# Seeding a PSUM bank from ScalarE and adding two matmul groups to it in one bank, in a fused Fourier mixing and gated feed-forward kernel

## The chip, the cores and the metric

The kernel runs on one core of one Trainium2 chip. The metric is the device time of one execution in microseconds (us). The kernel before took 1993.21 us, the median of three runs (1992.69 to 1993.93).

## The reference

```
X = np.fft.fft(x, axis=1); X = np.fft.fft(X, axis=2); attn_out = X.real     # x: (8, 3008, 256)
t = attn_out.reshape(8 * 3008, 256)
gate = 1 / (1 + exp(-(t @ w_gate)));  val = t @ w_val                       # (256, 1536) each
out = (gate * val) @ w_out                                                  # (1536, 256)
```

All data are float32. The real part of the two-dimensional transform has a symmetry that the kernel uses. With P the part made of cosines over both axes, Q the part made of sines over both axes, and E the part that comes from one feature column (the one in the middle), row k of a batch, times the weights, is P + E + Q, and row S - k is P + E - Q (S = 3008). So only 1505 rows of each batch are transformed, and each gives two rows of the result.

## The kernel before

**Weights.** The transform over the features is merged into the weights: for each of six pairs of blocks of 128 hidden features, `merge` multiplies the cosine table (`dt`) with a column block of w_gate or w_val in a PSUM bank (`ps`), and ScalarE copies the halves to `G2` and `G1`. Row 0 of `G2` is also sent by DMA into the small table `ge`, one column per block of 128 features; `ge` is the factor of E. The weights come as 64-bit numbers. `weight_parts` (two ScalarE operations) and `weight_join` (three VectorE operations and one on GpSimd, L236) turn a block of them into float32. `weight_load` brings the next block, and its buffer is that of an earlier block, so its DMA, which waits in the queue of SyncE, waits for that block's join. The `ge` transfers stand in the same queue behind it. `forms` makes seven combinations of the blocks of w_out, `wf`.

**Transform over the sequence.** For each batch, `half` sums products of a table of cosines or sines (`st`) with the folded input (`x`) into two PSUM banks, `ev` and `od`. ScalarE copies `ev` to `a` and `places` (VectorE) writes sums and differences of both to the rows of `pk` (P), `qk` (Q) and, for batch 0, `ek` (E). For batch 0 this is done ahead of the loop, with the groups of `cos` and `sin`. For batch b + 1 it is done in the middle of batch b (`whole`), at a unit where a chunk has just ended. E of batches 1 to 7 comes from `e_sums`, once.

**The main loop.** A batch's 1505 rows are cut into six chunks (five of 256 columns and one of 225). A chunk has six pairs, a pair has two blocks of 128 hidden features, and one block in one chunk is a unit: 8 x 6 x 12 = 576 units. A unit has three stages:

- `front` multiplies P by `G1` into bank `pa` and Q by `G2` into bank `pb`, gate and value side by side. VectorE computes `ae` = ge * ek + pa (L447, one operation for gate, one for value), then ae + pb for row k (L450) and ae - pb, in reversed order, for row S - k (L451), into `z`.
- ScalarE takes the sigmoid of the gate half of `z` (L672). `gate`, one unit later, multiplies gate and value into `h` (L462), and GpSimd makes sums of the parts of `h` in `s` (L464 to L468).
- `back`, two pairs later, multiplies `h` and `s` with `wf` into four PSUM banks `po`: seven products for a pair, three in its first unit and four in its second. At the end of a chunk ScalarE copies the four banks to `c` (L491, L549), GpSimd combines them, VectorE transposes (L509), and SyncE stores.

There are eight PSUM banks: a ring of four (pool `psx`) for `pa`, `pb`, `ps`, `ev`, `od` and `pe`, and four (`pso`) for `po`. The order of each engine's work is the order of the calls in the loop at the end of the kernel, written out by hand: `front` of a unit, `gate` of the unit before, `back`, the weight preparation (`pre`), the sigmoid, one step of the output work of the last chunk (`later`), and the rest of what is planned for that unit (`side`: joins, weight loads, merges, folds, transforms). Weight preparation fills the first units: units 0 to 8 each end with one merge, and the first `back` is that of unit 4. The `ps` of the merge for the gate of pair c stands in unit 2c - 3, that for its value in unit 2c - 2.

Of the kernel before, what the change touches and what calls it, by code (L numbers as in the profile page):

```python
# [42 lines left out]
NQ = 6  # L45
# [6 lines left out]
def kernel(  # L52
# [10 lines left out]
    nc = tc.nc  # L63
    B, _, _, _, D = xf.shape
    F = moe_w_gate.shape[1]
    P = 128
# [6 lines left out]
    NPR = NFT // 2  # L73
    CH = 256
# [15 lines left out]
    app = ctx.enter_context(tc.tile_pool(name="app", bufs=3))  # L90
    zp = ctx.enter_context(tc.tile_pool(name="zp", bufs=3))
# [3 lines left out]
    op = ctx.enter_context(tc.tile_pool(name="op", bufs=2))  # L95
    psx = ctx.enter_context(tc.tile_pool(name="psx", bufs=4, space=PSUM))
    pso = ctx.enter_context(tc.tile_pool(name="pso", bufs=1, space=PSUM))

    def mm(o, l, r, start, stop):
        nc.tensor.matmul(o, l, r, start=start, stop=stop, skip_group_check=True)  # L100
# [239 lines left out]
    PQE = {}  # L340

    def half(w, d, blk, sn, other=None):


        c0, n = ((0, NE), (NE, NO))[blk]
        ev, od = [bank(name, other and other[i])[:, 0:n] for i, name in enumerate(("ev", "od"))]

        def sums(*qs):
            for q in sorted(qs, key=lambda q: q % 2):
                mm((ev, od)[q % 2], w(q), ST[0][0:NP, int(sn), q, c0 : c0 + n], q < 2, q >= NQ - 2)  # L350

        def both():

            for r in range(2 - blk):
                for q in range(N3 if blk == 0 else NQ):
                    for par, sum_ in enumerate((ev, od)):
                        rows = slice(par * HP, par * HP + HP - 1 - (par and q % N3 == N3 - 1))
                        ks = slice(None) if blk else slice(r, n, 2)
                        wq = q if blk else q + N3 * (r ^ int(sn))
                        mm(sum_[:, ks], w(wq)[rows], ST[0][rows, int(sn), q, c0 : c0 + n][:, ks],  # L360
                           q == 0 and r == 0, q == (NQ if blk else N3) - 1)

        def then():
# [24 lines left out]
    def seq_group(b, blk, what, other=None):  # L388
        return half(lambda q: W[b, blk][what][:, q, :], PQE[b][what], blk, what == 1, other)
# [42 lines left out]
    def front(p, fh):  # L432
        b, c, i = pairs[p]
        k0, n = chunks[c]
        ks = slice(k0, k0 + n)
        f = 2 * i + fh
        fs = slice(f * P, (f + 1) * P)
        pk, qk, ek = PQE[b]
        pa = bank("pa").rearrange("p (g n) -> p g n", g=2)[:, :, 0:n]
        pb = bank("pb").rearrange("p (g n) -> p g n", g=2)[:, :, 0:n]  # L440
        for g in range(2):
            mm(pa[:, g], G1[:, g, fs], pk[:, ks], g == 0, True)
        for g in range(2):
            mm(pb[:, g], G2[:, g, fs], qk[:, ks], g == 0, True)
        ae = app.tile([P, 2, CH], F32, name="ae", tag="ae")[:, :, 0:n]
        for g in range(2):
            nc.vector.scalar_tensor_tensor(out=ae[:, g], in0=ek[:, ks], scalar=ge[:, g, f : f + 1],  # L447
                                           in1=pa[:, g], op0=ALU.mult, op1=ALU.add)
        z = zp.tile([P, 2, 2, CH], F32, name="z", tag="z")[:, :, :, 0:n]
        nc.vector.tensor_tensor(z[:, :, 0], ae, pb, op=ALU.add)  # L450
        nc.vector.tensor_tensor(z[:, :, 1, ::-1], ae, pb, op=ALU.subtract)  # L451
        return p, fh, z

    def gate(p, fh, z):

        n = chunks[pairs[p][1]][1]
        tt = nc.gpsimd.tensor_tensor
# [3 lines left out]
        h, s = H[p], SF[p]  # L461
        nc.vector.tensor_tensor(h[:, fh], z[:, 0], z[:, 1], op=ALU.mult)  # L462
# [14 lines left out]
    def back(p, part):  # L477
        b, c, i = pairs[p]
        n = chunks[c][1]
        if part == 0 and i == 0:  # L480
            PO[:] = [pso.tile([P, 2, CH], F32, name=f"po{t}", tag=f"po{t}") for t in range(4)]
        h, s = H[p], SF[p]
        move = {1: h[:, 0, 0], 2: h[:, 1, 0], 3: s[:, 3], 4: h[:, 1, 1], 5: s[:, 0], 6: s[:, 1],
                7: s[:, 2]}
        for m in ORDER[part]:
            t, j = SLOT[m]
            mm(PO[t][:, j, 0:n], wf[:, i, m - 1], move[m], i == 0 and m in FIRST,
               i == NPR - 1)
        if part == 0 and i == NPR - 1:
            PO.append(cp.tile([P, 7, CH], F32, name="c7", tag="c7"))  # L490
            nc.scalar.copy(PO[4][:, 6, 0:n], PO[3][:, 0, 0:n])  # L491
# [118 lines left out]
    def at(i, *fs):  # L610
        side.setdefault(i, []).extend(fs)

    def split(i, f, *args):

        at(i, lambda: at(i + 1, f(*args)))

    pre = {}
# [5 lines left out]
    for j in range(3, len(jobs)):  # L625
        w, c = jobs[j]
# [4 lines left out]
    i0 = 2 * NPR  # L631
# [7 lines left out]
    for i, f in enumerate(mirror_tables()):  # L639
        at(2 * i0 - 2 + i, f)  # L640
    at(3 * i0, e_fold)
    split(3 * i0 + 3, e_sums)
    at(3 * i0 + 5, table_again)

    for b in range(B - 1):
# [13 lines left out]
            for i, f in zip(calm(s0 if b else 3 * i0), mirror_x(b + 2)):  # L659
                at(i, f)  # L660

    fresh = None
    for i in range(2 * len(pairs)):
        done, fresh = fresh, front(i // 2, i % 2)
        if done is not None:
            gate(*done)
        if i >= 4:
            back(i // 2 - 2, i % 2)
        for f in pre.pop(i, []):
            f()  # L670
        z = fresh[2]
        nc.scalar.activation(z[:, 0], z[:, 0], AF.Sigmoid)  # L672
        if later:
            later.pop(0)()
        for f in side.pop(i, []):
            f()
    gate(*fresh)
    for f in later:
        f()
    del later[:]  # L680
# [54 lines left out]
```

## Time and profile before

| | |
|---|---|
| time, median of 3 | 1993.21 us |
| span in the profile | 1992.2 us |
| TensorE busy (matmul) | 1965.1 us, 99% |
| VectorE busy | 1777.8 us, 89% |
| GpSimd busy | 1348.3 us, 68% |
| ScalarE busy | 497.2 us, 25% |
| granted TensorE clock, mean | 0.996 |
| chain that ended last | TensorE 96% of the span |

A float32 product appears as two MATMUL records, each with its own LDWEIGHTS record. A record's time includes the drain after its last column, so the steps from one record's start to the next tell the real rate. The idle time in front of a group names what ended it. An engine other than the bound may idle at no cost. Busy time is a union over a stage whose parts have different limits, so the start (to about 103 us), the long middle and the tail are read apart.

### The profile page before, as it was taken

The numbers are of one execution on the slowest core, as the hardware profiler recorded it, in microseconds if no ns is written. First come the engines' busy times: TensorE is split into PE (matmuls) and PEld (weight loads), VectorE is DVE, ScalarE is ACT, GpSimd is POOL, SyncE is SP. The second block draws the span as 40 slices with busy tenths as digits, with TensorE's granted clock in tenths as the row PEclk, the third lists the DMA queues.
The fourth block names the chain that finished last, engine by engine and source line by source line (L and its number), as shares of the span: only waits on it lengthen the run. The fifth ranks groups of instructions, "written<-read, shape, count | busy, mean of one in ns | idle before, by whom it ended". The sixth has DMA issues, their size and how long they took to land.

```text
span 1992.2 us, 28166 instructions
## 1 busy us (share of the span) xinstructions
PE 1965.1 (99%) x9504; PEld 1737.3 (87%) x9504; DVE 1777.8 (89%) x3221; ACT 497.2 (25%) x876; POOL 1348.3 (68%) x1704
## 2 busy tenths in 40 slices
PE   6999999999999999999999999999999999999998
PEld 4888889888988889888898888988899888998888
DVE  7999979978999789997999979999799988898887
ACT  3422222222222222222222222222222222222221
POOL 3678867865787467874678646886478854655655
PEclk8999999999999999999999999999999999999999
DMA  7262421112020201202011020111200000000001
GB/s 265 85 134 77 154 90 48 48 27 75 16 66 25 82 19 23 73 11 90 17 44 46 17 90 17 43 47 32 75 11 12 21 27 11 11 20 12 11 17 26
DMA packets 160815, 100.33 MB, mean 50 GB/s; under 512 B 128419, under 2 KB 151715, under 8 KB 157994
## 3 DMA queue, kind: packets, MB, share of 16 engines
q1 hardware_dynamic: 158850, 98.00, 17.0%
q8 instruction: 76, 1.25, 0.3%
q10 hardware_dynamic: 1822, 0.54, 0.1%
q14 instruction: 67, 0.55, 0.1%
HBM read 73.74 MB, written 50.17 MB: 62 GB/s over the span
## 4 chain that ended last, share of the span: by engine, by line
PE 96%; DMA 2%; DVE 1%; ACT 0%; issue 0%; POOL 0%; SPq 0%; ACTq 0%; DVEq 0%; POOLq 0%
PE po L100 43%; PE pa L100 24%; PE pb L100 24%; PE ev L100 4%; DMA ge<-G 1%; DMA st<-in_stab_dram 1%; PE od L100 1%; PE ps L100 0%; DMA raw<-in_moe_w_val_dram 0%; DVE ae L447 0%; POOL wx L236 0%; PE pe L100 0%; DVE z L451 0%; DVE wx L232 0%; DVE os L509 0%
## 5 line engine op out<-in xcount | busy, mean ns | idle before, releaser
L672 ACT ACTIVATE z<-z 128x512 f32<-128x512 f32 (+1 forms) x576 | 358.5, 622 | 1297.5 <-DVE z L451 1297.5
L100 PE MATMUL pb<-qk,G 128*128 128x256 f32 (+1 forms) x2304 | 581.8, 375 | 2.5 <-DVE ae L447 2.5
L100 PE MATMUL pa<-pk,G 128*128 128x256 f32 (+1 forms) x2304 | 582.1, 375 | 0.0
L447 DVE SCALAR_TENSOR_TENSOR ae<-ek,ge,pa 128x256 f32<-128x256 f32 (+1 forms) x1152 | 488.1, 464 | 68.5 <-PE pa L100 65.0
L100 PE MATMUL po<-sf,wf 128*128 128x256 f32 (+1 forms) x2304 | 534.6, 375 | 0.0
L466 POOL TENSOR_TENSOR sf<-h 128x256 f32<-128x256 f32 (+1 forms) x288 | 206.9, 718 | 448.7 <-DVE h L462 448.7
L100 PEld LDWEIGHTS pb<-qk,G 128*128 128x128 f32 x2304 | 437.3, 190 | 53.6 <-DVE ae L447 4.0
L100 PEld LDWEIGHTS pa<-pk,G 128*128 128x128 f32 x2304 | 437.1, 190 | 51.7 <-issue 2.3
L100 PEld LDWEIGHTS po<-sf,wf 128*128 128x128 f32 x2304 | 437.7, 190 | 49.8 <-POOL sf L468 0.3
L462 DVE TENSOR_TENSOR h<-z 128x512 f32<-128x512 f32 (+1 forms) x576 | 480.6, 834 | 0.0
L450 DVE TENSOR_TENSOR z<-ae,pb 128x512 f32<-128x512 f32 (+1 forms) x576 | 390.1, 677 | 61.4 <-DVE ae L447 1.4
L100 PE MATMUL po<-h,wf 128*128 128x256 f32 (+1 forms) x1728 | 412.5, 375 | 0.0
L451 DVE TENSOR_TENSOR z<-ae,pb 128x512 f32<-128x512 f32 (+1 forms) x576 | 386.3, 671 | 0.0
L100 PEld LDWEIGHTS po<-h,wf 128*128 128x128 f32 x1728 | 328.3, 190 | 37.1
L464 POOL TENSOR_TENSOR sf<-h 128x256 f32<-128x256 f32 (+1 forms) x288 | 206.8, 718 | 96.4 <-DVE h L462 95.5
L468 POOL TENSOR_TENSOR sf<-h,sf 128x256 f32<-128x256 f32 (+1 forms) x288 | 207.8, 721 | 22.6
L467 POOL TENSOR_TENSOR sf<-sf,h 128x256 f32<-128x256 f32 (+1 forms) x288 | 207.7, 721 | 22.6
L100 PE MATMUL ev<-st,x 63*128 63x376 f32 (+4 forms) x372 | 98.5, 417 | 7.9 <-DVE x L290 5.9
L100 PEld LDWEIGHTS ev<-st,x 63*128 63x128 f32 (+1 forms) x372 | 66.5, 187 | 35.5 <-DVE x L290 6.3
L100 PE MATMUL od<-st,x 63*128 63x376 f32 (+4 forms) x372 | 97.4, 413 | 0.0
L549 ACT COPY c<-po 128x512 f32<-128x512 f32 (+1 forms) x141 | 75.5, 580 | 39.4 <-PE po L100 38.9
L509 DVE STREAM_TRANSPOSE os<-c 128x256 f32<-128x256 f32 x192 | 83.8, 436 | 0.2
(91 smaller groups left out, 830.2 us busy)
## 6 DMA issues: line engine op xcount, KB each, us to landing
x<-xr SPq DMA_DIRECT2D x14, 1536.0 KB
out_dram<-os SPq DMA_DIRECT2D x288, 64.0 KB
xr<-in_xf_dram SPq DMA_DIRECT2D x14, 768.0 KB
xr<-in_xf_dram SPq DMA_DIRECT2D x35, 256.0 KB
ek<-ed SPq DMA_DIRECT2D x7, 752.5 KB
out_dram<-os SPq DMA_DIRECT2D x92, 56.0 KB
x<-in_xf_dram SPq DMA_DIRECT2D x2, 1512.0 KB
tr<-in_stab_dram SPq DMA_DIRECT2D x2, 1129.5 KB
```

Source lines behind the costliest of these rows:

```text
L100: nc.tensor.matmul(o, l, r, start=start, stop=stop, skip_group_check=True)
L447: nc.vector.scalar_tensor_tensor(out=ae[:, g], in0=ek[:, ks], scalar=ge[:, g, f : f + 1], in1=pa[:, g], op0=ALU.mult, op1=ALU.add)
L450: nc.vector.tensor_tensor(z[:, :, 0], ae, pb, op=ALU.add)
L451: nc.vector.tensor_tensor(z[:, :, 1, ::-1], ae, pb, op=ALU.subtract)
L462: nc.vector.tensor_tensor(h[:, fh], z[:, 0], z[:, 1], op=ALU.mult)
L464: tt(s[:, 2], h[:, 0, 0], h[:, 0, 1], op=ALU.subtract)
L466: tt(s[:, 0], h[:, 0, 1], h[:, 1, 1], op=ALU.add)
L467: tt(s[:, 1], s[:, 0], h[:, 0, 0], op=ALU.subtract)
L468: tt(s[:, 3], h[:, 1, 0], s[:, 1], op=ALU.subtract)
L509: nc.vector.transpose(os_[:, s, 0:nb, h, :], t[:, slot, 0 : nb * TB])
L549: nc.scalar.copy(t[:, 2 * j : 2 * j + 2, 0:n], PO[j][:, :, 0:n])
L672: nc.scalar.activation(z[:, 0], z[:, 0], AF.Sigmoid)
```

## The change

Each unit now has one bank, `pf`, in place of `pa` and `pb`:

- `seed` writes ge * E into the bank, gate and value apart, ahead of time. For the first twelve units VectorE does it, one unit ahead; later ScalarE does, two units ahead.
- `front_a` adds the P part to the bank by matmul, without the flag that starts a sum.
- `twice` (ScalarE) reads the bank, which now holds P + E, and writes two times it to `ae`.
- `front_b` adds the Q part, so that the bank holds the row k: P + E + Q.
- `gate_a` and `gate_b`, one unit later: ScalarE takes the sigmoid of the bank's gate half, VectorE computes ae minus the bank, which is P + E - Q, the row S - k, in reversed order, and multiplies the first row's gate and value, the value straight from the bank. Then ScalarE takes the second sigmoid and VectorE multiplies the second row.

TensorE's order in a unit is now `front_a`, `back`, `front_b` in place of pa, pb, `back`. [...] So the first batch's sums get two small extra matmuls per group (eight in all), and the later transforms and `e_sums` move from the ring to the product banks `po`. What the change is for: the work of VectorE on each unit shrinks, and ScalarE, which is mostly idle, takes a part of it.

```diff
-        ev, od = [bank(name, other and other[i])[:, 0:n] for i, name in enumerate(("ev", "od"))]
+        full = [bank(name, other and other[i]) for i, name in enumerate(("ev", "od"))]
+        ev, od = [sum_[:, 0:n] for sum_ in full]
...
+            if other is None and NQ - 1 in qs:
+                for sum_ in full:
+                    mm(sum_[:, n:], dt[:, 0, 0:P], dt.rearrange("p c d -> p (c d)")[:, n:], False, True)
...
-        _, then, both = seq_group(b, blk, what)
+        _, then, both = seq_group(b, blk, what, (2, 1) if what else (3, 0))
...
-        ps = bank("pe")
+        ps = bank("pe", 3)
...
+    def seed(i):
+        (_, _, ek), ks, n, f, _ = cut(i)
+        PF[i] = bank("pf").rearrange("p (g n) -> p g n", g=2)[:, :, 0:n]
+        for g in range(2):
+            if i < 2 * NPR:
+                nc.vector.tensor_scalar(out=PF[i][:, g], in0=ek[:, ks],
+                                        scalar1=ge[:, g, f : f + 1], scalar2=None, op0=ALU.mult)
+            else:
+                nc.scalar.activation(PF[i][:, g], ek[:, ks], AF.Copy, scale=ge[:, g, f : f + 1])
+    def front_a(i):
+            mm(PF[i][:, g], G1[:, g, fs], pk[:, ks], False, True)
+    def twice(i):
+        nc.scalar.activation(AP[i], PF[i], AF.Copy, scale=2.0)
+    def front_b(i):
+            mm(PF[i][:, g], G2[:, g, fs], qk[:, ks], False, True)
...
+        nc.scalar.activation(z[:, 2], pf[:, 0], AF.Sigmoid)
+        nc.vector.tensor_tensor(z[:, 0:2, ::-1], AP.pop(i), pf, op=ALU.subtract)
+        nc.vector.tensor_tensor(H[p][:, fh, 0], z[:, 2], pf[:, 1], op=ALU.mult)
...
+        nc.scalar.activation(z[:, 0], z[:, 0], AF.Sigmoid)
+        nc.vector.tensor_tensor(h[:, fh, 1], z[:, 0], z[:, 1], op=ALU.mult)
...
-    split(3 * i0 + 3, e_sums)
+    at(3 * i0 + 3, lambda: e_sums()())
...
+    count = 2 * len(pairs)
+    seed(0)
+    for i in range(count):
+        front_a(i)
+        if i:
+            gate_a(i - 1)
+        twice(i)
+        if i:
+            gate_b(i - 1)
+        if i >= 4:
+            back(i // 2 - 2, i % 2)
+        front_b(i)
+        for f in pre.pop(i, []):
+            f()
+        for j in range(i + 1, min(count, i + 3)) if i >= i0 else (i + 1,) if i + 1 < i0 else (i0, i0 + 1):
+            if j not in PF:
+                seed(j)
+        if later:
+            later.pop(0)()
+        for f in side.pop(i, []):
+            f()
```

More of the change, by code (lines that the diff above doesn't have):

```diff
@@ L430, with cut @@
     H, SF = {}, {}
-    def front(p, fh):
-        b, c, i = pairs[p]
+    def cut(i):
+        b, c, _ = pairs[i // 2]
         k0, n = chunks[c]
[L435 to L440, printed above, removed]
-        for g in range(2):
-            mm(pa[:, g], G1[:, g, fs], pk[:, ks], g == 0, True)
-        for g in range(2):
-            mm(pb[:, g], G2[:, g, fs], qk[:, ks], g == 0, True)
-        ae = app.tile([P, 2, CH], F32, name="ae", tag="ae")[:, :, 0:n]
-        for g in range(2):
[L447 to L452, printed above, removed]
@@ L454, in gate @@
-    def gate(p, fh, z):
-        n = chunks[pairs[p][1]][1]
-        tt = nc.gpsimd.tensor_tensor
+        f = i % (2 * NPR)
+        return PQE[b], slice(k0, k0 + n), n, f, slice(f * P, (f + 1) * P)
+    PF, AP, Z = {}, {}, {}
+    def seed(i):
+        (_, _, ek), ks, n, f, _ = cut(i)
+        PF[i] = bank("pf").rearrange("p (g n) -> p g n", g=2)[:, :, 0:n]
+        for g in range(2):
+            if i < 2 * NPR:
[3 more added lines that the diff above has]
+                nc.scalar.activation(PF[i][:, g], ek[:, ks], AF.Copy, scale=ge[:, g, f : f + 1])
@@ new lines, in front_a, with gate_a @@
+    def front_a(i):
+        (pk, _, _), ks, _, _, fs = cut(i)
+        for g in range(2):
+            mm(PF[i][:, g], G1[:, g, fs], pk[:, ks], False, True)
+    def twice(i):
+        n = cut(i)[2]
+        AP[i] = app.tile([P, 2, CH], F32, name="ae", tag="ae")[:, :, 0:n]
+        nc.scalar.activation(AP[i], PF[i], AF.Copy, scale=2.0)
+    def front_b(i):
+        (_, qk, _), ks, _, _, fs = cut(i)
+        for g in range(2):
+            mm(PF[i][:, g], G2[:, g, fs], qk[:, ks], False, True)
+    def gate_a(i):
+        n = cut(i)[2]
+        p, fh = i // 2, i % 2
+        z = Z[i] = zp.tile([P, 3, CH], F32, name="z", tag="z")[:, :, 0:n]
@@ L460, in gate, with gate_b @@
             SF[p] = sp.tile([P, 4, CH], F32, name="sf", tag="sf")[:, :, 0:n]
-        h, s = H[p], SF[p]
-        nc.vector.tensor_tensor(h[:, fh], z[:, 0], z[:, 1], op=ALU.mult)
+        pf = PF.pop(i)
+        nc.scalar.activation(z[:, 2], pf[:, 0], AF.Sigmoid)
+        nc.vector.tensor_tensor(z[:, 0:2, ::-1], AP.pop(i), pf, op=ALU.subtract)
+        nc.vector.tensor_tensor(H[p][:, fh, 0], z[:, 2], pf[:, 1], op=ALU.mult)
+    def gate_b(i):
+        p, fh = i // 2, i % 2
+        z, h, s = Z.pop(i), H[p], SF[p]
+        tt = nc.gpsimd.tensor_tensor
+        nc.scalar.activation(z[:, 0], z[:, 0], AF.Sigmoid)
+        nc.vector.tensor_tensor(h[:, fh, 1], z[:, 0], z[:, 1], op=ALU.mult)
         if fh == 0:
@@ L611, in at @@
         side.setdefault(i, []).extend(fs)
-    def split(i, f, *args):
-        at(i, lambda: at(i + 1, f(*args)))
     pre = {}
@@ L660 @@
                 at(i, f)
[L662 to L666, printed above, removed]
+    count = 2 * len(pairs)
[7 more added lines that the diff above has]
+            gate_b(i - 1)
         if i >= 4:
             back(i // 2 - 2, i % 2)
+        front_b(i)
         for f in pre.pop(i, []):
             f()
-        z = fresh[2]
-        nc.scalar.activation(z[:, 0], z[:, 0], AF.Sigmoid)
+        for j in range(i + 1, min(count, i + 3)) if i >= i0 else (i + 1,) if i + 1 < i0 else (i0, i0 + 1):
+            if j not in PF:
+                seed(j)
         if later:
@@ L676 @@
             f()
-    gate(*fresh)
+    gate_a(count - 1)
+    gate_b(count - 1)
     for f in later:
```

## The prediction

> **What bounds the kernel now.** I read the busy totals first, then four stretches of the span, then two pieces of the timeline, and last the groups with shapes kept apart, for durations.
>
> ```profile
> PE 1965.1 (99%) x9504; PEld 1737.3 (87%) x9504; DVE 1777.8 (89%) x3221; ACT 497.2 (25%) x876; POOL 1348.3 (68%) x1704
> ```
> ```profile
> core 0: us, PE busy (x) PEld busy (x) DVE busy (x) ACT busy (x) POOL busy (x), PEclk, DMA share, GB/s
> 0.00:51.00 51.00, 33.79 (x95) 21.14 (x96) 37.48 (x56) 16.31 (x29) 19.77 (x20) 0.90 0.78 259
> 51.00:103.00 52.00, 49.53 (x226) 42.17 (x225) 47.16 (x80) 25.94 (x59) 35.11 (x45) 1.00 0.32 97
> 103.00:1984.00 1881.00, 1881.00 (x9183) 1673.54 (x9182) 1689.53 (x3077) 454.91 (x788) 1293.43 (x1641) 1.00 0.15 43
> ```
> TensorE is the bound. From 103 to 1984 us it is busy in all of 1881 us. A busy PE need not be at its peak, so I look at the steps:
> ```profile
> 701.95 1.03 PE L100 MATMUL pa<-pk,G 128*128 128x256 f32 x4
> 702.81 1.03 PE L100 MATMUL pb<-qk,G 128*128 128x256 f32 x4
> 703.67 1.46 PE L100 MATMUL po<-h,wf 128*128 128x256 f32 x6
> ```
> Four records of pa take 702.81 - 701.95 = 0.86 us, so a record is 0.216 us and a product (two records) 0.432; pb takes the same, and six of po 1.30. The 1.03 holds the last record's drain of about 0.16. Nothing stands between the groups: the steady part is a gapless queue of matmuls, and the change removes no matmul. The only slack is before 103 us, and the tail behind the last matmul. In the start two things show:
> ```profile
> 68.70 0.37 SPq L214 DMA_DIRECT2D wx<-in_moe_w_gate_dram  x1
> 69.17 1.11 SPq L255 DMA_DIRECT2D ge<-G  x2
> ...
> 72.84 0.48 DVE L447 SCALAR_TENSOR_TENSOR ae<-ek,ge,pa 128x256 f32<-128x256 f32 x1 [1.30 <-DMA ge<-G]
> ```
> ```profile
> 63.54 0.35 ACT L252 COPY G<-ps 128x256 f32<-128x256 f32 x1
> ```
> The copy that makes this ge's source ended at 63.9, but the ge transfer was issued at 69.17, since the queue of SyncE stood behind a weight load waiting for its buffer (the waits of that queue list L214 on POOL wx L236, 16.9 us in 4 waits). It landed 2.1 to 2.5 us after its issue ended. VectorE, a whole unit behind TensorE there, waited 1.30 us, and through it TensorE. First pairs of units 0 and 12 start at 51.24 and 103.13; the matmuls between are 48.4 us, so the start loses 3.5 us here. Durations:
> ```profile
> L672 ACT ACTIVATE z<-z 128x512 f32<-128x512 f32 x480 | 302.7, 631 | 1094.0 <-DVE z L451 1094.0
> L549 ACT COPY c<-po 128x512 f32<-128x512 f32 x120 | 65.6, 587 | 38.1 <-PE po L100 37.6
> L491 ACT COPY c<-po 128x256 f32<-128x256 f32 x40 | 14.8, 369 | 40.6 <-PE po L100 40.6
> L450 DVE TENSOR_TENSOR z<-ae,pb 128x512 f32<-128x512 f32 x480 | 330.1, 688 | 51.4 <-DVE ae L447 1.4 <-PE po L100 0.5
> L447 DVE SCALAR_TENSOR_TENSOR ae<-ek,ge,pa 128x256 f32<-128x256 f32 x960 | 412.1, 469 | 63.4 <-PE pa L100 60.5 <-DMA ge<-G 1.8
> ```
>
> [...]
>
> **The change part by part.** A unit (one block of 128 hidden features, one chunk) is now: pair A (P part) 0.86 us, three or four products of back 1.30 or 1.73, pair B (Q part) 0.86. B waits for ScalarE's doubling of the bank.
>
> VectorE loses per unit 2 x 0.469 + 0.688 + 0.681 + 0.82 = 3.1 us and gets one 512-wide subtraction 0.68 and two 256-wide products of about 0.42[...]: 1.5 us. VectorE does not bound the steady part, so this is worth nothing there.
>
> ScalarE loses one sigmoid (0.63) and gets sigmoid a (PSUM, 256) 0.40, doubling 0.62 (587[...]), sigmoid b 0.42, and two seeds. No row shows a write of ScalarE into PSUM. [...] Bounds: 0.40, like sigmoid a, and 0.62, like a 512-wide one. I take 0.49. Sum 2.42 us in units of 3.02 and 3.46: it fits.
>
> Steady unit, t = 0 at A: A's stream ends 0.86, ScalarE sees it 0.20 later, doubles to 1.68. B is due at 2.16, and needs its release 0.16 before (in the trace pb's weights started 0.05 after the release, and its second record 0.32 after that instead of 0.22). Slack 0.32, with n = 225 0.19. VectorE's subtraction (0.63 to 1.3) is done before sigmoid b.
>
> End of a chunk (unit 3): doubling to 1.68, sigmoid b 2.00, three copies of po one per 0.49 to 3.47, seeds to 4.4, sigmoid a 4.7, doubling of the next unit to 5.22; its B is due at 3.46 + 0.86 + 1.30 = 5.62 less 0.16. Slack 0.24, at the narrow chunk 0.04. With seeds at the upper bound of 0.62 it loses up to 0.1 per chunk, or 0.3 if every ScalarE term is long. I book 0.5 us in all; the matmuls of back hide the rest.
>
> Transform in product banks: it starts behind the last product and the copies of po, banks 3 and 0 long copied; evacuations fall under its own matmuls (3.8 and 1.9 us a group). 0. The sums of E now sit in bank 3, which the next unit's first product needs: two copies, VectorE's two placements (0.53 each) and a third copy end 2.2 us behind them, that product comes after 0.86: +1.4 us, once.
>
> The start, step by step. The eight extra matmuls are bound by their weight loads (2 x 0.19 us each). Four fall into the 2.02 us in which TensorE waits for the sine table, four add 1.5 us. Seed 0 needs the last placement of Q (52.25) and two VectorE operations of 0.47: A of unit 0 starts 0.5 late. Units 0 to 3 have no back between A and B, so B waits 0.20 + 0.62 + 0.16 = 0.98: 3.9 us. In unit 1 the table load and sigmoid a stand ahead of the doubling: +1.25. Then ge: seed i+1 is now needed before A, where before only the lagging VectorE used it. For unit 4: the units start at 53.25, 57.7, 63.4 (57.7 plus two pairs 1.73, merge 1.73, wait 0.98 and 1.25), 67.8 and 72.3. In unit 2 VectorE's subtraction waits for sigmoid a, which stands behind the merge's copies until 64.5; subtraction and product to 65.6, sigmoid b 65.75, product 66.2, seeds of unit 3 to 67.1, the join's three operations (0.5, 0.75, 0.8 by rows L231, L232, L234, with 0.04 between) to 69.1. GpSimd has the join of unit 1 until 66.0, four forms to 68.4, three sums of 0.73 to 70.8 and this join of 1.28 to 72.2. SyncE then issues the weight load (0.4) and ge (1.1) to 73.7, landing 75.8, second seed 76.3; A was due at 72.3: +4.2. For unit 6 the same chain from VectorE's 82.8: load 86.3, ge 87.4, landing 89.5, seed 90.0, due 86.4: +3.7. Units 10 and 11 (ge of the last pair, no load ahead): +1.0 and +0.5. Queued behind the waiting seed on VectorE are the joins, which is why the loss comes back at unit 6. Sum: 1.5 + 0.5 + 3.9 + 1.25 + 4.2 + 3.7 + 1.5 = 16.6; the 3.5 us of before go: +13.1.
>
> The tail stays within 0.3 us: B is closer to the end, its chain (sigmoid a, subtraction, sigmoid b, product, two sums: 3.5 us) against ten products of 0.38. Total: 13.1 + 1.4 + 0.5 = +15, so **2008.5 us**.
>
> **Rivals.** (1) ScalarE becomes the bound at each chunk's end: every term at its long end gives 0.3 us at some 41 ends, +12: about 2021. For it: slack of only 0.04 to 0.24, and an unseen PSUM write. Against: it catches up within a unit. (2) The ge chain is shorter, because VectorE has less to do and joins end earlier: without the 4.2 and 3.7, 2000.5. For it: VectorE's load in the start falls. Against: GpSimd's queue and B's wait set the join, not VectorE's load. (3) Faster: A, back, B hides all waits and the relieved VectorE removes the 3.5 us: 1989.7. For it: VectorE was the cause of those waits. Against: units 0 to 3 have nothing to put between A and B, and nothing else in the span is idle. (4) No change: start gains and losses cancel, 1993.
>
> **How the numbers follow.** Forecast 0.70, rival 1 0.13, rival 2 0.09, rival 3 0.04, rival 4 0.04. The range goes from rival 2 to rival 1: 2000 to 2022. It leaves out rivals 3 and 4 and the ends of the others. Slower by over 0.2% (above 1997.2) takes the first three: 0.92; within 0.2% 0.04; faster 0.04.
>
> **What would show it.** Right: ScalarE at about 1400 us busy, VectorE near 1000, TensorE still back to back from about 118 us; the first steady pair of unit 12 near 116 to 118 instead of 103; waits of PE pf on ACT ae in units 0 to 3, and of PE pf on VectorE's seeds at units 4 and 6, those on DMA ge; a wait of about 1.4 us near the sums of E. Wrong: pf waiting for ACT ae at every chunk's end (rival 1), unit 12 before 108 us (rivals 2 and 3), or waits of po on ACT a in the transforms, which I cost at nothing.

## The result, and the profile after

| | before | after |
|---|---|---|
| time, median of 4 runs each | 1992.95 us (1992.54 to 1993.93) | 2009.28 us (2008.67 to 2012.23) |
| span in the profile | 1992.2 us | 2006.7 us |

The ratio is 1.0084, with a 95% interval of 1.0067 to 1.0102: the kernel became slower by 0.8%. The medians differ by 16.3 us; the two profiled executions, from which the rest of this section is read, differ by 14.5. The busy totals of the kernel after, engine by engine:

```profile
PE 1971.3 (98%) x9520; PEld 1740.7 (87%) x9520; DVE 1093.4 (54%) x2093; ACT 1332.4 (66%) x3156; POOL 1285.5 (64%) x1704
```

VectorE lost 684 us of work and ScalarE took 835 us more. The change did to these engines what it was meant to do, and the time went up. TensorE has 16 records more, the eight extra matmuls, so it wasn't given more work worth 14 us. It waits more, and the next view says where. These are three stretches of the kernel after, cut as those of before were: busy time of each engine, granted clock, DMA share.

```profile
core 0: us, PE busy (x) PEld busy (x) DVE busy (x) ACT busy (x) POOL busy (x), PEclk, DMA share, GB/s
0.00:51.00 51.00, 35.17 (x112) 22.73 (x113) 38.56 (x59) 16.97 (x31) 19.69 (x20) 0.93 0.79 267
51.00:118.00 67.00, 57.43 (x241) 47.41 (x242) 44.09 (x85) 38.87 (x93) 40.78 (x55) 0.95 0.29 86
118.00:1998.00 1880.00, 1877.43 (x9164) 1669.66 (x9162) 1006.60 (x1940) 1276.61 (x3033) 1224.96 (x1630) 1.00 0.15 43
```

From 118 us TensorE is busy in all but 2.6 of 1880 us; in the 67 us ahead of that it idles for 9.6 us, and the granted clock there is 0.95. To place the loss to a tenth of a microsecond I take the start of the first P pair of certain units as marks (t0 for unit 0 and so on). A is the P pair of a unit (`front_a`), B its Q pair (`front_b`):

| | t0 | units 0 to 12 | 12 to 39 | 39 to 40 | 40 to 48 | 48 to 575 | unit 575 to the last matmul |
|---|---|---|---|---|---|---|---|
| before | 51.24 | 51.89 | 87.20 | 5.56 | 26.00 | 1754.13 | 8.38 |
| after | 51.00 | 63.50 | 87.20 | 5.56 | 29.11 | 1754.14 | 8.44 |
| difference | -0.24 | +11.61 | 0 | 0 | +3.11 | +0.01 | +0.06 |

The whole difference of 14.5 us lies in two places: the first twelve units, and the units behind the sums of E. Units 48 to 575, with all seven transforms in the product banks, take the same time to 0.01 us. Where the slack was forecast to be smallest, in the unit behind the last copies of a chunk (unit 88), the timeline of the kernel after has:

```profile
373.26 1.03 PE L102 MATMUL pf<-pk,G 128*128 128x256 f32 x4
374.12 1.46 PE L102 MATMUL po<-h,wf 128*128 128x256 f32 x6
374.32 0.60 ACT L467 ACTIVATE ae<-pf 128x512 f32<-128x512 f32 x1
375.42 1.03 PE L102 MATMUL pf<-qk,G 128*128 128x256 f32 x4
```

A starts at 373.26, back 0.86 later, and B 1.30 after that, so TensorE has no gap. ScalarE's doubling ends at 374.92, 0.50 before B. Of the start I read the waits first. Each line names an instruction, what it waited for, the sum in us, how often, and the longest one:

```profile
PE pf L102 <- DVE pf L453: 6.0, 5, 3.1
PE pf L102 <- ACT ae L467: 5.2, 5, 2.0
```

Matmuls of `pf` wait for VectorE's seed (L453) and for the doubling (L467), five times each. All but one of these fall into the units before unit 12; the last is that of the sums of E. Two pieces of the timeline show the two kinds. First, units 0 and 1:

```profile
51.00 1.10 PE L102 MATMUL pf<-pk,G 128*128 128x256 f32 x4 [0.70 <-DVE pf L453]
52.20 0.60 ACT L467 ACTIVATE ae<-pf 128x512 f32<-128x512 f32 x1 [1.21 <-PE pf L102]
52.85 1.13 PE L102 MATMUL pf<-qk,G 128*128 128x256 f32 x4 [0.75 <-ACT ae L467]
53.82 1.89 PE L102 MATMUL ps<-ws,dt 128*128 128x256 f32 x8
...
56.40 1.28 ACT L483 ACT_TABLE_LOAD   x1
57.97 0.59 ACT L467 ACTIVATE ae<-pf 128x512 f32<-128x512 f32 x1
58.62 1.49 PE L102 MATMUL pf<-qk,G 128*128 128x256 f32 x4 [2.04 <-ACT ae L467]
59.90 3.26 PE L102 MATMUL ps<-ws,dt 128*128 128x256 f32 x8
```

In unit 0 B (52.85) stands idle until the doubling is through. In unit 1 the load of the sigmoid's table (1.28, as long as in the kernel before, where it started at 54.64) stands ahead of the doubling and the wait grows to 2.04. The last line shows something else: the same eight records of a merge took 1.89 at 53.82 and 3.26 at 59.90. Then unit 4:

```profile
70.45 0.37 SPq L216 DMA_DIRECT2D wx<-in_moe_w_gate_dram  x1
70.93 1.11 SPq L257 DMA_DIRECT2D ge<-G  x2
...
74.60 0.49 DVE L453 TENSOR_SCALAR pf<-ek,ge 128x256 f32<-128x256 f32 x1 [3.49 <-DMA ge<-G]
75.14 1.13 PE L102 MATMUL pf<-pk,G 128*128 128x256 f32 x4 [3.11 <-DVE pf L453]
76.11 2.55 PE L102 MATMUL po<-h,wf 128*128 128x256 f32 x6
```

The `ge` transfer leaves SyncE's queue behind the weight load, ending at 72.04, and VectorE's seed starts 2.56 later; A of unit 4 comes behind that. Behind A, six records of `po` again take 2.55 where a steady chunk needs 1.46. Both long groups are one thing, a lower clock. Here is the granted clock in a window inside the first of them, below a window of ordinary speed for comparison (columns as above; the last section has a window of the second):

```profile
53.80:55.50 1.70, 1.70 (x9) 1.50 (x8) 1.13 (x3) 0.13 (x1) 0.37 (x1) 1.00 0.17 31
59.90:62.50 2.60, 2.60 (x8) 2.06 (x7) 2.13 (x5) 0.96 (x3) 0.81 (x2) 0.50 0.01 3
```

Behind 59.3 and again behind 76.3 the clock is at half for 3.4 us, and a record takes 0.427 us instead of 0.216. TensorE is then busy but slow, which no view of busy time or waits shows as a loss.

The sums of E, in the timeline of the kernel after:

```profile
209.48 0.47 ACT L429 COPY a<-pe 7x376 f32<-7x376 f32 x1 [1.12 <-DVE er L380]
210.00 1.56 PE L102 MATMUL po<-h,wf 128*128 128x256 f32 x6 [1.60 <-ACT a L429]
210.45 0.53 DVE L380 TENSOR_TENSOR er<-a 7x376 f32<-7x376 f32 x1
211.01 0.54 ACTq L431 DMA_DIRECT2D ed<-er  x1
211.60 0.38 ACT L483 ACTIVATE z<-pf 128x256 f32<-128x256 f32 x1 [1.65 <-DVE er L380]
211.88 0.59 ACT L467 ACTIVATE ae<-pf 128x512 f32<-128x512 f32 x1
212.53 1.13 PE L102 MATMUL pf<-qk,G 128*128 128x256 f32 x4 [0.96 <-ACT ae L467]
```

Two waits stand here. The product (210.00) waits for the bank, as forecast. B (212.53) waits for the doubling, which wasn't: ScalarE had nothing to compute from 209.95 to 211.60. Its queue held the DMA that sends `er` away, and this DMA waited for VectorE's last placement (210.45 to 210.98), with sigmoid a and the doubling behind it.

### The profile page after: what moved, and what is told of

The parts are those of the page before. It is cut to its first block, busy times and chain, and to the rows that moved or that the text cites. A ratio compares the mean times of both kernels' runs of the same rounds, so it can differ in the third digit from the quotient of the medians.

```text
span 2006.7 us, 27514 instructions
## 1 busy us (share of the span) xinstructions
PE 1971.3 (98%) x9520; PEld 1740.7 (87%) x9520; DVE 1093.4 (54%) x2093; ACT 1332.4 (66%) x3156; POOL 1285.5 (64%) x1704
## 4 chain that ended last, share of the span: by engine, by line
PE 96%; DMA 2%; DVE 1%; ACT 1%; issue 0%; ACTq 0%; DVEq 0%
PE pf L102 48%; PE po L102 42%; PE ev L102 4%; DMA ge<-G 1%; PE ps L102 1%; DMA st<-in_stab_dram 1%; PE od L102 0%; DVE pf L453 0%; DMA raw<-in_moe_w_gate_dram 0%; DVE z L484 0%; ACT ae L467 0%; PE pe L102 0%; ACT z L492 0%; ACT G L254 0%; ACT z L483 0%
## 5 line engine op out<-in xcount | busy, mean ns | idle before, releaser
L484 DVE TENSOR_TENSOR z<-ae,pf 128x512 f32<-128x512 f32 (+1 forms) x576 | 389.6, 676 | 615.3 <-ACT z L483 615.2
L102 PE MATMUL pf<-pk,G 128*128 128x256 f32 (+1 forms) x2304 | 582.7, 375 | 6.0 <-DVE pf L453 6.0
L102 PE MATMUL pf<-qk,G 128*128 128x256 f32 (+1 forms) x2304 | 582.9, 375 | 5.2 <-ACT ae L467 5.2
L456 ACT ACTIVATE pf<-ek,ge 128x256 f32<-128x256 f32 (+1 forms) x1128 | 532.1, 472 | 18.3
L467 ACT ACTIVATE ae<-pf 128x512 f32<-128x512 f32 (+1 forms) x576 | 339.2, 589 | 248.2 <-PE pf L102 248.1
L102 PEld LDWEIGHTS pf<-pk,G 128*128 128x128 f32 x2304 | 436.7, 190 | 59.3 <-DVE pf L453 7.0
L102 PEld LDWEIGHTS pf<-qk,G 128*128 128x128 f32 x2304 | 438.0, 190 | 57.0 <-ACT ae L467 7.2
L493 DVE TENSOR_TENSOR h<-z 128x256 f32<-128x256 f32 (+1 forms) x576 | 348.1, 604 | 190.4 <-ACT z L492 188.6
L492 ACT ACTIVATE z<-z 128x256 f32<-128x256 f32 (+1 forms) x576 | 233.1, 405 | 17.4 <-DVE z L484 17.3
L485 DVE TENSOR_TENSOR h<-z,pf 128x256 f32<-128x256 f32 (+1 forms) x576 | 235.1, 408 | 0.0
```

The source lines that it names most:

```text
L456: nc.scalar.activation(PF[i][:, g], ek[:, ks], AF.Copy, scale=ge[:, g, f : f + 1])
L467: nc.scalar.activation(AP[i], PF[i], AF.Copy, scale=2.0)
L484: nc.vector.tensor_tensor(z[:, 0:2, ::-1], AP.pop(i), pf, op=ALU.subtract)
L485: nc.vector.tensor_tensor(H[p][:, fh, 0], z[:, 2], pf[:, 1], op=ALU.mult)
L493: nc.vector.tensor_tensor(h[:, fh, 1], z[:, 0], z[:, 1], op=ALU.mult)
```

## The experiments

My theory at this point: the loss of the start is made of B's waits behind the doubling in units 0 to 3, of the waits for `ge`, and of the slow clock that follows long idle times; the loss of the sums is made of the bank and of ScalarE's queue. Since t0 moved between 50.6 and 62.2 from one execution to another (last section), the runs are read from unit 0 on, by the segments of the table above. Four runs were timed in rounds and have an interval; the times of the others are single executions.

**The order of the queue of SyncE.** The planned calls of a unit are registered in another order, so that the `ge` transfer is issued ahead of the weight load. The second run also loads the sigmoid's table before anything needs it.

```diff
         at(j - 9, lambda j=j: weight_join(j))
-        if KEEP <= j < len(jobs) - 3:
-            at(j - 9, lambda j=j: weight_load(j + 3))
     for j in range(3, len(jobs)):
         w, c = jobs[j]
         at(2 * c + (-3, -2, 1)[w], lambda j=j: weight_use(j))
+    for j in range(KEEP, len(jobs) - 3):
+        at(j - 9, lambda j=j: weight_load(j + 3))
```

> The changed kernel with merge, and so the ge transfers, called ahead of the weight load in each unit's side work. Theory (seeds 4 and 6 wait for ge, which stands behind a weight load in SyncE's queue): the waits of TensorE on VectorE's seed, 3.3 us before unit 4 and 2.0 before unit 6, fall under 0.7 each; the half-rate stretch of 1.7 us that follows the first disappears too; unit 12 starts near 107.5 in place of 114.5 and the time is about 2002. Rival (VectorE as a whole is too slow in the start): the waits only change their releaser, unit 12 stays within 2 us of 114.5.

And on top of it, at the head of the kernel:

```diff
+    early = const.tile([2, 1, 1], F32, name="early")
+    nc.scalar.activation(early, zero[:, :, 0:1], AF.Sigmoid)
```

> As the run before, and one sigmoid of two elements as ScalarE's first operation, so that the table with the sigmoid is loaded in the first microseconds instead of in unit 1. Theory: B of unit 1 waits 1.0 us instead of 2.3, and the half-rate stretch after it (1.5 us) disappears, so unit 12 starts 2.5 to 3 us earlier than in the run before and the time is about 1999. Rival (the half rate has another cause than the idle time before it): the wait falls by 1.3, the half-rate matmuls stay.

Units 0 to 12 took 56.37 us with the order changed, 7.1 less than after, and 53.40 with the table early as well, another 3.0 less, as both expectations had it. The whole times were 2012.66 and 1999.64; the first is far from the 2002 expected because its t0 was at 62.2, which is no effect of the order (TensorE waited 14.5 us for the tables `st` ahead of t0). The waits of the two kernels' B and A, the order alone first:

```profile
PE pf L102 <- ACT ae L467: 5.2, 5, 2.0
PE pf L102 <- DVE pf L453: 1.1, 3, 0.7
```

```profile
PE pf L102 <- ACT ae L467: 3.9, 5, 1.0
PE pf L102 <- DVE pf L453: 1.1, 3, 0.7
```

A's waits fell from 6.0 to 1.1: those of units 4 and 6 are gone, without anything removed from any engine. The early table took 1.3 off B's longest wait, and no slow stretch followed in this run, which is the other 1.7 of the 3.0. So the wait for `ge` came from what stood ahead of it in its queue. With both edits B still waits about 0.9 in each of units 0 to 3.

**The same order in the kernel before.** The edit is the same.

> The kernel before with merge called ahead of the weight load. If ge behind a weight load also costs the kernel before something: its waits of pb on VectorE (0.96, 1.65 and 0.36 us at units 4, 5 and 7) fall, unit 12 starts 1 to 2.5 us earlier than 103.13, time about 1991. If VectorE's own load makes those waits: unchanged within 0.5 us.

The time was 1993.41 us, ratio 0.9994 (0.9985 to 1.0002) to the unchanged kernel in the same rounds, whose median there was 1995.1; units 0 to 12 took 50.52 instead of 51.89, 1.4 less. The gain is there in the trace and too small to tell in the time. In the kernel before the same queue cost 1.4 us, in the kernel after 7.1 with what followed, since there the seed stands in front of TensorE.

**The eight extra matmuls alone**, put into the kernel before:

```diff
+            if other is None and NQ - 1 in qs:
+                for sum_ in full:
+                    mm(sum_[:, n:], dt[:, 0, 0:P], dt.rearrange("p c d -> p (c d)")[:, n:], False, True)
```

> The kernel before with nothing added but the eight extra matmuls of the first batch's sums. The prediction's term: four of them lie in the wait for the sine table, four add 1.5 us to the start of unit 0. Theory now: the four that lie in the wait also shorten TensorE's idle time from 2.5 us to under 1, so it isn't slowed to half rate from 41 to 45 us; that gives back what the other four add, and unit 0 starts within 0.5 us of 51.24. Rival: unit 0 starts 1.3 to 1.7 us later.

It took 1995.32 us, and t0 was 52.56, which missed: the table of sines came 2.1 us later in this execution. From the first sum with sines to t0 it took 10.32 us, and in the kernel before 11.09. The first six records of these sums, in the timeline of this kernel:

```profile
42.24 2.14 PE L100 MATMUL ev<-st,x 126*128 126x377 f32 x6 [1.19 <-DMA st<-in_stab_dram]
```

and in that of the kernel before:

```profile
40.15 3.00 PE L100 MATMUL ev<-st,x 126*128 126x377 f32 x6 [2.02 <-DMA st<-in_stab_dram]
```

The same six records take 2.14 instead of 3.00. Before, TensorE idles for 2.02 in front of them, and the clock goes to half at 41.3, for 3.4 us; with the extra matmuls it idles for 1.19 and the clock stays up: 2.14 is what these six records take in the kernel after as well, from 39.82, at a granted clock of 1.00. The four extra matmuls in the sine part take 0.23 each, 0.9 in all, and still the stretch is 0.8 shorter, so the clock is worth 1.7, half of 3.4. Of the eleven kernels here that have the extra matmuls, the clock fell at this place in two; of the two without, in both. So they shorten the wait and don't rule the fall out.

**Matmuls between A and B.** Each merge of units 0 to 8 is called ahead of `front_b` (on top of the two edits above, with the sums of E as in the next part):

```diff
-        at(2 * c + (-3, -2, 1)[w], lambda j=j: weight_use(j))
+        uses.setdefault(2 * c + (-3, -2, 1)[w], []).append(lambda j=j: weight_use(j))
...
             back(i // 2 - 2, i % 2)
+        for f in uses.pop(i, []):
+            f()
         front_b(i)
```

> The changed kernel with four edits: merge called between back and pair B, so that its four products stand between A and B in units 0 to 8 (this also puts ge ahead of the weight load), the table load at the start, and the sums of E in the ring in two parts. Theory (the changed kernel loses in the start and at the sums of E alone): unit 12 starts between 101.5 and 105 us, the limit being VectorE, whose seeds and joins take 3.9 to 4.4 us a unit against 3.5 on TensorE in units 0 to 3; time 1991 to 1995, equal to the kernel before within 0.1%. Rival (something in the steady part is slower too): over 2000.

It took 2003.77 us (five rounds, ratio 1.0045, 1.0032 to 1.0058), and units 0 to 12 took 56.46: 3 us more than without this edit. Both texts missed. The start is slower than the theory had it, and the rival has the number (over 2000) but not the reason: units 48 to 575 took 1754.18, so nothing is lost in the steady part. Its timeline in the start:

```profile
60.38 1.00 DVE L454 TENSOR_SCALAR pf<-ek,ge 128x256 f32<-128x256 f32 x2
61.43 1.13 PE L102 MATMUL pf<-pk,G 128*128 128x256 f32 x4 [1.27 <-DVE pf L454]
```

B has no wait left in the start, but A now waits up to 1.5 us, in seven units (6.5 us in all by the waits). The seeds stand in VectorE's queue behind the joins and behind the subtraction and products of the unit before, and these came later. The wait moved from one engine to another. So the queue of VectorE has to be put in order too: in the next run `seed` of the next unit stands right behind `twice`, ahead of the second product of the unit before; `weight_parts` (`pre`), whose result the joins need, is called ahead of the merge; and the sums of E are those of the second form below.

```diff
         twice(i)
+        if i + 1 < i0:
+            seed(i + 1)
...
-        front_b(i)
-        for f in pre.pop(i, []):
+        for f in pre.pop(i, []) + uses.pop(i, []):
             f()
+        front_b(i)
```

> The run before, and the merge's four products between A and B of units 0 to 8, this time with the weight preparation called ahead of the merge (so that ScalarE does it while TensorE merges) and the seed of the next unit ahead of the second product of the last one. Theory (the earlier filled start lost on VectorE, whose seeds stood behind joins and sigmoid b, 1.4 us a unit): the waits of 0.98 us in units 0 to 3 go, the seeds wait under 0.3 us, unit 0 to 12 takes 49.5 to 51.5 us, and the time is 0 to 2.5 us below the kernel before. Rival (VectorE's work in the start is too much in any order): unit 0 to 12 over 53.4.

Units 0 to 12 took 52.01 us, 0.1 more than in the kernel before, and the time was 1996.93 us (ratio 1.0015, 1.0007 to 1.0023). Most of the loss is gone, but the theory missed: it had the kernel faster than before, and it is slower by 0.15%. B waits nowhere in the start. What is left behind t0 are three waits of A, of 1.5, 0.7 and 0.9 us, in units 4, 6 and 10. The trace says what they wait for. Ahead of units 4 and 10 VectorE has no time left: it is busy for 9.27 of the 9.48 us up to the end of unit 4's seed, and for 9.69 of the 9.90 us up to unit 10's. Ahead of unit 6 the seed waits 1.42 us for `ge` once more. So the rival text holds in part: at two of the three places VectorE's own work is what TensorE waits for.

**The sums of E.** First with the sums in the ring again, where one product with zeros takes the place of the start flag, and the second half of the work a unit later:

```diff
-        ps = bank("pe", 3)
+        ps = bank("pe")
+        mm(ps, dt[0:2, 0, 0:P], zero[:, 0], True, True)
...
-                       ST[0][0:NP, 0, q + par, c0 : c0 + n], q == 0, q == NQ - 2)
+                       ST[0][0:NP, 0, q + par, c0 : c0 + n], False, q == NQ - 2)
...
-    at(3 * i0 + 3, lambda: e_sums()())
+    at(3 * i0 + 3, lambda: at(3 * i0 + 4, e_sums()))
```

> The changed kernel with the sums of E back in the ring of four banks and cut in two as before; one zero product over the whole bank takes the place of the start flag[...]. Theory (the loss is made of single events, and one is the bank that the sums of E share with the next unit's first product): the stretch from unit 40 to unit 48, 29.1 us in the changed kernel, falls to 26.0 to 26.4, the zero product adds up to 0.9 ahead of it, and the time falls by 2.2 to 3.1 us, to about 2006.5. Rival (that stretch loses because ScalarE runs late after a chunk's end): no change in it.

Units 40 to 48 took 28.04 us and 39 to 40 6.62: together 34.66, where the kernel after takes 34.67, and the time was 2008.19. Neither text had that. The product's wait for the bank is gone, as the theory had it; the product with zeros and a longer wait elsewhere take up what that gained. B of unit 41 starts 1.94 late, and the timeline of this kernel says why:

```profile
212.91 1.06 DVE L380 TENSOR_TENSOR er<-a 7x376 f32<-7x376 f32 x1
...
214.01 0.54 ACTq L432 DMA_DIRECT2D ed<-er  x1
214.60 0.38 ACT L484 ACTIVATE z<-pf 128x256 f32<-128x256 f32 x1 [2.21 <-DVE er L380]
```

The DMA in ScalarE's queue waits for the placement, which itself took 1.06 this time instead of 0.53, and ScalarE's work on the unit waits behind it. The second form takes product bank 1, does the first placement with the first copies, and issues the DMA two units later:

```diff
-        ps = bank("pe", 3)
+        ps = bank("pe", 1)
...
+        places(er, 0, True, a, ps[at_(0, 0), 0:NE])
...
-            places(er, 0, True, a, ps[at_(0, 0), 0:NE])
...
-            nc.scalar.dma_start(out=ed, in_=er)
+            return lambda: nc.scalar.dma_start(out=ed, in_=er)
...
-    at(3 * i0 + 3, lambda: e_sums()())
+    at(3 * i0 + 3, lambda: at(3 * i0 + 4, lambda rest=e_sums(): at(3 * i0 + 5, rest())))
```

> The changed kernel with the sums of E in product bank 1, which the next unit does not write, and their evacuation in three steps, one a unit: two copies and the first placement, then the last copy and placement, then the DMA, which in the changed kernel stood in ScalarE's queue waiting for VectorE. Theory (two waits make the loss: the next unit's first product for bank 3, and ScalarE's doubling behind the DMA issue): 40 to 48 falls from 29.1 to 26.0 to 26.3 us, time 3 us below the changed kernel. Rival (only the bank matters): it falls by 1.9, to 27.2.

Units 40 to 48 took 26.95: 2.2 of the 3.1 us are gone (the whole time, 2009.36 with t0 at 53.8, does not tell it), so neither text of the expectation had it right. B of unit 40, ahead of which the DMA had stood, waits for nothing now; B of unit 42 starts 0.85 late instead. The DMA's issue is hardly the reason for that: in the timeline of this kernel the issue (218.05 to 218.59) lies beside the seeds, which end at 218.52, and the sigmoid follows at 218.63. Ahead of that ScalarE idles for 1.84 us for VectorE's subtraction (216.53), which stands behind the two last placements, of 1.09 and 1.06 instead of 0.53. With the order, the early table and these sums together:

> The early table load, ge ahead of the weight load, and the sums of E as in the run before. Unit 0 to 12 as with the first two alone, 53.4 us, 40 to 48 26.1, all else as in the changed kernel: 1.5 us above the kernel before (51.9 and 26.0), so 1994 to 1995, a ratio of 1.0005 to 1.001. Rival (the parts are not additive): over 1997.

1997.69 us (ratio 1.0016, 1.0009 to 1.0023); the segments are 53.42 and 26.95, so the gains add, though the time is over the rival's 1997. The expectation had counted from 1993; the kernel before had a median of 1995.1 in these rounds.

**The steady part: how much room has ScalarE?** One more ScalarE operation in each unit from unit 12 on, which copies `ae` onto itself:

```diff
             gate_b(i - 1)
+        if i >= i0:
+            nc.scalar.copy(AP[i], AP[i])
```

> The changed kernel with one more ScalarE copy per unit from unit 12 on (the doubled bank onto itself, 128x512[...]), which no matmul waits for directly. The prediction's slack at a chunk's end is 0.24 us, at the narrow chunk 0.04, and 0.3 to 0.6 within a chunk. Theory: B of the unit after a chunk's end waits 0.2 to 0.5 us at some 39 ends, time 8 to 20 us above the changed kernel, with TensorE waiting for ae. Rival (ScalarE's work is hidden with room to spare): no more than 2 us.

The time was 2022.16 us, as the theory had it; units 48 to 575 took 1766.39, 12.25 more. Its timeline in the same unit 88:

```profile
376.90 0.59 ACT L467 ACTIVATE ae<-pf 128x512 f32<-128x512 f32 x1
...
377.54 1.13 PE L102 MATMUL pf<-qk,G 128*128 128x256 f32 x4
...
378.07 0.60 ACT L699 COPY ae<-ae 128x512 f32<-128x512 f32 x1
```

B follows the end of the doubling by 0.05. At 37 chunk ends B's pair comes late: at 23 of them by 0.29 us, at the seven where narrow units begin by 0.38, and at the seven behind a narrow chunk by 0.46; between them nothing is lost. In the kernel after the doubling of such a unit ends 1.66 us behind A's start, and here 2.28. It comes 0.62 later and costs 0.29, so the room was 0.33 us; for the narrow units it was 0.54 - 0.38 = 0.16. The lines of the kernel after say the same: to lose nothing B needs the end of the doubling 0.16 ahead (the 0.05, and 0.11 that its second record loses otherwise), and there it is 0.50 ahead.

**The seeds on VectorE throughout:**

```diff
-            if i < 2 * NPR:
+            if True:
                 nc.vector.tensor_scalar(out=PF[i][:, g], in0=ek[:, ks],
```

> The changed kernel with all seeds on VectorE, which takes about 1 us a unit from ScalarE and gives it to VectorE (1.5 to 2.5 us of 3.0 to 3.5). Theory (matmuls bound the steady part and both engines fit beneath): stretch from unit 48 to 575 stays at 1754.1 us within 1 us and the time within 2 us of the changed kernel. Rival (ScalarE holds TensorE back somewhere): that stretch becomes shorter.

Units 48 to 575 took 1754.14 us, as after, and the whole kernel 2009.43, as the theory had it. Its busy totals:

```profile
PE 1969.8 (98%) x9520; PEld 1740.4 (87%) x9520; DVE 1579.0 (79%) x3221; ACT 866.8 (43%) x2028; POOL 1280.5 (64%) x1704
```

486 us more on VectorE and 466 less on ScalarE change nothing: neither engine bounds this part.

**What the slow clock costs in the start.** Three runs that leave the first units as they are after answer this, since the clock didn't fall at the same places in each. Times from t0, and idle times in front of A:

| | after | seeds on VectorE | one more on ScalarE |
|---|---|---|---|
| slow stretch in unit 1 | yes | no | yes |
| A of unit 4: idle; start | 3.27; 24.14 | 4.82; 24.01 | 3.24; 24.12 |
| slow stretch behind it | yes | yes | no |
| A of unit 6: idle; start | 1.98; 37.84 | 2.51; 37.93 | 3.52; 37.67 |
| units 0 to 12 | 63.50 | 63.59 | 63.34 |

Where the slow stretch is missing, the wait for `ge` behind it is longer by just about what the stretch takes (4.82 against 3.27, 3.52 against 1.98), and A starts when it did. The waits for `ge` end at a time that TensorE doesn't set, and the slow matmuls are hidden in front of them. Behind t0 a slow stretch cost something only where the `ge` waits were gone (1.7 of the 3.0 us between the first two runs of this section).

## Why the prediction was right, step by step

| term | forecast, us | measured, us |
|---|---|---|
| extra matmuls, and A of unit 0 late | 1.5 + 0.5 | -0.8 + 0.9 |
| B in units 0 to 3 | 3.9 | 4.0 |
| table load ahead of the doubling | 1.25 | 1.3 |
| A of unit 4 behind `ge` | 4.2 | 5.0 |
| A of unit 6 behind `ge` | 3.7 | 3.7 |
| A of units 10 and 11 | 1.5 | 1.0 |
| less what before lost | -3.5 | -3.5 |
| sums of E | 1.4 | 3.1 |
| steady | 0.5 | 0 |
| transforms, tail | 0 | 0.06 |
| sum | +15 | +14.8 |

The marks gave 14.5 for this sum of 14.8: in the kernel after the first sum with sines started 0.33 us earlier (39.82 against 40.15), which is none of the change's doing. From there to t0 it takes 11.18 us, before 11.09, so the first line is 0.1 in all. How the measured terms come out: each wait is how much later a group's first record starts than in a gapless queue (so it holds about 0.16 of drain that the waits of the profile leave out), and another 0.11 that its second record then takes longer (0.91, 0.85, 0.91 and 0.91 for B; the unit with the table load 2.21, less 0.91). For A of units 4 and 6 the gap (3.27 and 1.98) is taken together with the 1.6 us that the slow stretch in front of it cost, since the comparison above shows that the two stand for one wait. One sum of the prediction is off by itself: 15.0 on top of 1993.21 is 2008.2, not 2008.5.

**Right:** TensorE stayed the bound; relieving VectorE was worth nothing; the start carries the loss; the doubling that nothing hides (0.20 + 0.62 + 0.16) is measured as 0.85 to 0.91 and 0.11. VectorE's subtraction (L484) did wait for sigmoid a, to which 615.2 us of its idle time are put down, at no cost. The chain of the join, the weight load and `ge` was forecast with A of unit 4 at 76.5 - 53.25 = 23.25 behind t0, and it came at 24.14. The early runs confirm it: with `ge` ahead of the load those waits vanish. That ScalarE keeps up at a chunk's end was the difference between forecast and rival 1; it held with more room than forecast, 0.34 us instead of 0.24, and 0.16 instead of 0.04 in the narrow chunk, because the doubling isn't late there at all. A seed on ScalarE took 476 ns and the doubling 597; the 0.49 and 0.62 us of the prediction were its author's estimates. These groups of the kernel after, shapes kept apart, have the durations on which the slack rests (busy us, mean ns, idle before):

```profile
L456 ACT ACTIVATE pf<-ek,ge 128x256 f32<-128x256 f32 x936 | 445.8, 476 | 15.2
L467 ACT ACTIVATE ae<-pf 128x512 f32<-128x512 f32 x480 | 286.6, 597 | 214.1 <-PE pf L102 214.1
L493 DVE TENSOR_TENSOR h<-z 128x256 f32<-128x256 f32 x480 | 287.5, 599 | 162.4 <-ACT z L492 160.6
```

**Mis-sized, and nearly cancelling.** Of the start, the extra matmuls: they take 0.23 us each, not the 0.38 of their weight loads, so the four that fill no wait cost 0.9 and not 1.5. The other four fill a wait as forecast, and the clock, which fell there before, stayed up; that pays for the four others and for most of A of unit 0, late by 0.9. So unit 12 started at 114.5, earlier than the 116 to 118 that the prediction named. The clock had no place in the prediction. In the kernel after its two falls behind t0 cost nothing of their own only because the waits for `ge` stand behind them. The two waits of `ge` sum to 8.7 where 7.9 was forecast. The forecast let GpSimd's queue decide when unit 3's join ends. That is so with the seeds on VectorE throughout, where no slow stretch delays unit 2; in the kernel after GpSimd idles for 0.68 us ahead of that join, and VectorE's last part of it, ended at 69.01, decides. "The sums of E now sit in bank 3 ... +1.4 us, once" is the term with the largest error: the bank cost 1.9 (0.1 of it in the record behind the wait), and the other 1.2 is a wait that the forecast didn't look for. It followed only the consumers of the bank, not the queue of the engine that copies: the DMA issue in ScalarE's queue waits for VectorE and holds back sigmoid and doubling. Of the two products of a unit on VectorE, both estimated at 0.42 us, the first (L485) took 413 ns and the second (L493) 599; the second hid, as the idle time in front of it on that line shows. Measured against forecast, the first line of the table came out 1.9 lower, the sums of E 1.7 higher, the waits for `ge` 0.8 higher, and the steady part with units 10 and 11 1.0 lower. That the sum fits so closely is luck; that it is made of these waits is not.

**The rivals.** Rival 1 would have needed B to wait at each chunk's end in the kernel after. It happened only when 0.61 us more (607 ns for 512 elements, L699) were put on ScalarE in each unit, and then gave 2022.16, near its 2021. Rival 2 took the waits for `ge` to vanish with VectorE's load; they vanished only with the order of the queue. The rivals on the other side had VectorE's relief for their reason, which had no wait to remove.

**Stays open:** whether a form of the change exists that beats before. From t0 to the last matmul the fully ordered form takes 1934.4 us (52.01 + 87.25 + 5.56 + 26.95 + 1754.18 + 8.45), the kernel before 1933.2, and the kernel before with `ge` ahead of the load, which is the fair comparison, 1931.8. No form of the change that was tried beats either.

## What to carry to other kernels

Before relieving an engine, ask which wait of the bounding engine ends with it: here there was none in 1880 us, and 684 us less on VectorE gave nothing there. An accumulation that passes through another engine between two matmul groups (A, doubling, B) here cost that engine's whole latency where nothing stood between them (0.85 to 0.91 us a unit in units 0 to 3) and nothing in units 48 to 575, so its price is set by the start and the seams, not by the steady part. And for every value that moves from a lagging engine in front of TensorE, follow each queue it passes, DMA issues among them: a transfer or an issue that waits held what stood behind it (here the sigmoid behind the DMA of `er`, for 1.65 us), and a small reorder of a queue (7 us here) can be worth more than the arithmetic that was moved.

## What was not expected of the hardware

The clock fell to half after short idle times. Idle times of 2.2 us in front of B of unit 1 were followed, 0.3 to 1.4 us after TensorE's restart, by 3.4 us at half rate in five of six runs, and those of 3.2 to 4.8 us in front of A of unit 4 in four of five (in one of these already during the wait); those of 1.9 to 3.5 us in front of A of unit 6 in none of five. None of 0.9 or 1.5 us in these units was followed by it. So 2.2 us were enough most times, and 3.5 once were not: the length of the wait alone doesn't tell.

Two runs show that on waits of the same length. Behind the 3.27 us in front of A of unit 4, the kernel after has this stretch (columns as in the views above):

```profile
76.32:79.73 3.41, 3.41 (x9) 2.69 (x8) 3.22 (x7) 2.13 (x4) 2.92 (x5) 0.50 0.20 19
```

and behind the 3.24 us in front of the same A, the kernel with one more operation on ScalarE has these two:

```profile
76.80:78.20 1.40, 1.40 (x9) 1.22 (x8) 1.40 (x3) 0.78 (x2) 0.68 (x1) 1.00 0.00 0
79.05:80.70 1.65, 1.65 (x9) 1.47 (x8) 1.58 (x5) 0.52 (x1) 1.57 (x4) 1.00 0.32 37
```

The first runs at half clock and the other two at full. What decides whether the clock falls was not shown.

The time t0 of the first unit moved by more than most of what was measured here: 50.6 to 54.5 us in all runs but one, where the tables came late and it was 62.2. The kernel before took 1992.0 to 2002.0 us in the 41 runs beside the last experiments. Effects of 1 to 3 us in the start are told from such noise only by marks inside the trace.
